# Attention scores of a pooled-attention and MLP kernel: 64 pools by one matmul for both token kinds, 8 pools in column tiles, k through a transposing DMA

## The chip, the cores and the metric

The kernel runs on one core of a Trainium2 chip. The metric is device time in microseconds (us), median of the runs of one program; a profile gives in addition the span from the first to the last instruction, about 1.8 us less. A core has TensorE (PE; the loads of its stationary operand, `lhsT` in the code, are shown apart, as PEld), VectorE (DVE), ScalarE (ACT), GpSimd (POOL) and SyncE (SP, which issues DMAs). A `q` after an engine's name (SPq, POOLq) stands for the DMA issues in its queue.

## The reference

Eight batches of eight heads, 576 tokens, head dimension 64. Keys and values are averaged over groups of eight tokens (72 pools), each token attends to the 72 pools of its head, and the result, 4608 tokens of 512, goes through an MLP with a tanh-gelu.

```python
k_p = k.reshape(B, H, Sp, pool, D).mean(axis=3)        # pool = 8, Sp = 72
v_p = v.reshape(B, H, Sp, pool, D).mean(axis=3)
scores = (1/sqrt(D)) * matmul(q, k_p.transpose(0, 1, 3, 2))
attn = softmax(scores)
x = matmul(attn, v_p)                                   # then to [B*S, H*D]
out = gelu_tanh(x @ w_in) @ w_out                       # 512 -> 2048 -> 512
```

## The kernel before

The nine groups of 512 tokens of the MLP run one after the other on TensorE. Each group has a first stage, 64 matmuls with w_in whose results, in banks of PSUM (the memory that these matmuls write), ScalarE takes through gelu, and a second stage, 64 matmuls with w_out. The attention of the next batch is woven into the second stage. Even and odd tokens lie in the two halves of the partitions of qT (64 rows of the head dimension each), so a score matmul takes pooled keys that are zero in the other half: 2 token kinds x 8 heads = 16 score matmuls a batch.

```python
def qk(b, c, pr, bank):                     # c: token kind, pr: pair of heads
    for e in range(2):
        h = 2 * pr + e
        n = pool_rows(pr)                   # 72 or 128
        nc.tensor.matmul(out=PS[:n, bank + e, :CH]...,          # CH = 288 tokens
                         lhsT=kTs[b % 2][c][:, h, :n],
                         rhs=qTs[b][:, h // 4, :, h % 4 * 32:h % 4 * 32 + 32], ...)

def trans_k(b, bank):                       # pooled k: five transposes by TensorE,
    trans_k_mm(b, bank)                     # then twelve copies by VectorE
    for e in range(2):
        trans_k_copy(b, e, bank)
# ... cut: exponentials (ACT), av (values, 16 matmuls), norm (ln, ln, exp), mult
```

The softmax here doesn't subtract the row's maximum and nothing guards it: scores larger than these inputs give would overflow.

## Time and profile before

| | before |
|---|---|
| median of 3 runs | 308.13 us |
| profiled span | 306.1 us |
| TensorE busy, mean granted clock | 97%, 1.00 |
| one period (first stage + second stage), batch 3 to batch 5 | 31.84 us |
| of it second stage (attention woven in) | 17.75 us |
| start of the second w_in stage to the end | 250.3 us |

The lines behind this are in the prediction below. A "period" is read from the chain that ended last, printed in order of time: it turns from the line of the w_in matmuls to the line of the w_out matmuls once in each period.

### The profile page before, as it was taken

Reading aid. Unit: us, or ns where it says so; the run is one execution under the profiler, and the core shown is the slowest. Engines: PE = TensorE matmul, PEld = TensorE weight load, DVE = VectorE, ACT = ScalarE, POOL = GpSimd, SP = SyncE. Lnnn points to the kernel's source line nnn. Section 1 sums busy time; section 2 is a strip of 40 time slices with the busy share of each in tenths; the row PEclk is TensorE's granted clock in tenths of the full one; section 3 lists DMA queues with packets and bytes.
Section 4 is the critical chain, followed back from the end, with each engine's and each line's share of the span. In section 5 each row is a group of like instructions: output and inputs, shape, how many; then the busy total and the mean of one; then the engine's idle time right before and its main releaser. Section 6 shows DMA issues by size and latency. Waiting matters only on the chain.

```text
span 306.1 us, 4354 instructions
## 1 busy us (share of the span) xinstructions
PE 296.8 (97%) x1528; PEld 157.6 (51%) x1557; DVE 150.5 (49%) x336; ACT 219.0 (72%) x402; POOL 35.0 (11%) x67
## 2 busy tenths in 40 slices
PE   8999899999999999999999999999999999999994
PEld 3555455555555555555555555555555555445543
DVE  5885757572577057805682559245932630120012
ACT  1687489867987798779977898789868986206500
POOL 7102002305003200320014000400000000000000
PEclk9999999999999999999999999999999999999999
DMA  7999987977955962696159827672101210121022
GB/s 221 266 254 264 227 171 139 310 168 184 257 138 113 278 154 53 118 279 154 35 112 250 181 61 103 203 153 71 35 1 36 59 44 0 36 70 35 2 68 69
DMA packets 30806, 41.12 MB, mean 134 GB/s; under 512 B 18176, under 2 KB 18432, under 8 KB 29888
## 3 DMA queue, kind: packets, MB, share of 16 engines
q0 software_dynamic: 7568, 24.38, 33.7%
q1 hardware_dynamic: 22528, 15.14, 21.1%
q10 hardware_dynamic: 688, 1.31, 1.3%
q8 instruction: 12, 0.20, 0.3%
q14 instruction: 10, 0.08, 0.1%
HBM read 36.70 MB, written 9.44 MB: 151 GB/s over the span
## 4 chain that ended last, share of the span: by engine, by line
PE 87%; DMA 11%; issue 1%; ACT 0%; DVE 0%; POOLq 0%
PE PS L344 40%; PE PS L335 37%; DMA qb<-in_q_dram 11%; PE PS L238 5%; PE PS L260 4%; PE PS L173 1%; PE PS L203 0%; ACT e L246 0%; ACT ld L268 0%; ACT ld L267 0%; DVE osb L353 0%; POOLq L550 0%
## 5 line engine op out<-in xcount | busy, mean ns | idle before, releaser
L344 PE MATMUL PS<-w_out_b,gT 128*128 128x512 bf16 (+2 forms) x577 | 133.9, 373 | 0.7
L335 PE MATMUL PS<-xT,w_in_b 128*128 128x512 bf16 x563 | 126.6, 379 | 0.7
L341 ACT ACTIVATE gT<-PS 128x512 bf16<-128x512 f32 x144 | 81.2, 603 | 48.1 <-PE PS L335 48.0
L335 PEld LDWEIGHTS <-w_in_b 128*128 128x128 bf16 x576 | 64.7, 113 | 57.2
L344 PEld LDWEIGHTS <-gT 128*128 128x128 bf16 x592 | 57.0, 97 | 55.7 <-issue 0.4
L353 DVE COPY osb<-PS 128x512 f32<-128x512 f32 (+2 forms) x37 | 25.1, 677 | 98.2 <-PE PS L344 78.6
L278 DVE TENSOR_TENSOR xT<-PS,rc 64x288 bf16<-64x288 f32 x112 | 50.9, 455 | 31.7 <-ACT rc L270 27.5
L246 ACT ACTIVATE e<-PS 72x576 bf16<-72x576 f32 (+1 forms) x64 | 41.0, 647 | 8.8 <-PE PS L238 7.9
L238 PE MATMUL PS<-qT,kT 128*72 128x288 bf16 (+1 forms) x128 | 25.8, 286 | 0.9 <-ACT qT L213 0.6
L270 ACT ACTIVATE rc<-ld 128x288 f32<-128x288 f32 x56 | 24.8, 444 | 1.8
L313 ACT ACT_TABLE_LOAD x17 | 21.8, 1283 | 4.3 <-issue 4.1
L267 ACT ACTIVATE ld<-PS 64x288 f32<-64x288 f32 x56 | 22.8, 408 | 1.3
L268 ACT ACTIVATE ld<-PS 64x288 f32<-64x288 f32 x56 | 22.5, 402 | 1.4
L260 PE MATMUL PS<-e,vp 72*128 72x288 bf16 (+1 forms) x112 | 23.1, 286 | 0.0
L138 DVE TENSOR_TENSOR kt<-kt 128x1280 f32<-128x1280 f32 (+5 forms) x18 | 18.9, 1048 | 7.6 <-DMA kt<-in_v_dram 4.6
L238 PEld LDWEIGHTS <-kT 128*72 128x72 bf16 (+1 forms) x128 | 13.2, 105 | 15.1 <-DVE qT L215 1.2
L453 POOL COPY gate<-qT 1x2 bf16<-1x2 bf16 x6 | 1.0, 174 | 138.5 <-DMA qT<-qb 138.5
L138 DVE TENSOR_TENSOR vt<-vt 128x1024 f32<-128x1024 f32 (+1 forms) x16 | 15.3, 956 | 1.7 <-DMA vt<-in_v_dram 1.4
L183 DVE COPY kT<-PS 64x288 bf16<-64x288 bf16 (+2 forms) x48 | 13.0, 318 | 6.2 <-PE PS L173 6.0
L260 PEld LDWEIGHTS <-vp 72*128 72x128 bf16 (+1 forms) x112 | 11.0, 98 | 3.8
L365 PE MATMUL PS<-idle 128*128 128x512 bf16 x32 | 10.4, 468 | 1.6 <-DVE idle L126 1.2
L76 POOL DMA_DIRECT2D kt<-in_v_dram x14 | 8.0, 586 | 0.1
(48 smaller groups left out, 88.8 us busy)
## 6 DMA issues: line engine op xcount, KB each, us to landing
out_dram<-osb SPq DMA_DIRECT2D x140, 64.0 KB
kt<-in_k_dram POOLq DMA_DIRECT2D x7, 1024.0 KB, 6.0
vt<-in_v_dram POOLq DMA_DIRECT2D x12, 512.0 KB, 8.7
qb<-in_q_dram POOLq DMA_DIRECT2D x7, 576.0 KB, 11.8
w_in_b<-in_moe_w_in_dram POOLq DMA_DIRECT2D x2, 1024.0 KB, 16.8
w_out_b<-in_moe_w_out_dram POOLq DMA_DIRECT2D x4, 512.0 KB, 19.3
vt<-in_v_dram SPq DMA_DIRECT2D x3, 512.0 KB
kt<-in_k_dram POOLq DMA_DIRECT2D x7, 128.0 KB, 6.0
```

The costliest lines, as they stand in the source:

```text
L138: nc.vector.tensor_tensor(out=o, in0=a, in1=b, op=ALU.add)
L238: nc.tensor.matmul(out=PS[:n, bank + e, :CH].rearrange("j (t p) -> j t p", p=32), lhsT=kTs[b % 2][c][:, h, :n], rhs=qTs[b][:, h // 4, :, h ...
L246: nc.scalar.activation(out=e[:n], in_=PS[:n, bank:bank + 2, :CH], func=ACT.Exp, scale=1.0 / 64.0)
L260: nc.tensor.matmul(out=PS[:, bank + x, :CH], lhsT=window(vps[b % 2][:n], 2 * pr + x), rhs=e[:n, x, :], start=True, stop=True)
L267: nc.scalar.activation(out=ld[0:64], in_=PS[64:128, bank, :CH], func=ACT.Ln)
L268: nc.scalar.activation(out=ld[64:128], in_=PS[0:64, bank + 1, :CH], func=ACT.Ln)
L270: nc.scalar.activation(out=rc, in_=ld, func=ACT.Exp, scale=-1.0)
L278: nc.vector.tensor_tensor(out=xT[rows, pr, col:col + CH], in0=PS[rows, bank + x, :CH], in1=rc[rows], op=ALU.mult)
L335: nc.tensor.matmul(out=PS[:, h_bank(g, fo), c0:c1], lhsT=w_in_b[fo // 8][:, ko, q * 512 + j:(q + 1) * 512:4], rhs=xT[:, ko, r0 + c0:r0 + c ...
L341: nc.scalar.activation(out=gTs[g][:, fo, :], in_=PS[:, h_bank(g, fo), :], func=ACT.Gelu_apprx_tanh)
L344: nc.tensor.matmul(out=PS[:, bank, c0:c1], lhsT=gTs[g][:, fo, r * 128:(r + 1) * 128], rhs=w_out_b[:, fo, c0:c1], start=(fo == 0), stop=(fo ...
L353: nc.vector.tensor_copy(out=osb[:, c0:c1], in_=PS[:, bank, c0:c1])
```

## The change

In batches 2 to 7 one stationary tile of 128 columns holds 64 pools of a head twice, for even and for odd tokens, so one matmul gives both: 8 in place of 16. The last 8 pools of all heads and both kinds, the remainder, come from eight matmuls of 16 rows. Four of them write to four column tiles (outputs that start at rows 0, 32, 64 and 96), meant to run side by side. Their exponentials must end up in rows 64 to 71 below the 64 others; VectorE moves the even rows, a DMA the odd ones. The pooled k is transposed by a DMA, not by TensorE.

```diff
+    KX = 2
+    def trans_k_dma(b):
+        kxs[b] = bp.tile([128, 2 * H + 2, 64], BF16, name="kx", bufs=1)
+        nc.sync.dma_start_transpose(out=kxs[b], in_=kz.rearrange("p h e c -> p (h e c)"))
+    def rem_scores(b):
+        kf = kxs[b].rearrange("p b j -> p (b j)")
+        for h in range(H):
+            i, x = h % 4, h // 4
+            nc.tensor.matmul(out=PS[32 * i:32 * i + 16, 6 + x, :CH].rearrange("j (t p) -> j t p", p=32),
+                             lhsT=kf[:, 2 * H * 64 + h::H], rhs=qTs[b][:, x, :, 32 * i:32 * i + 32],
+                             start=True, stop=True)
+    def rem_expo(b):
+        r = ep.tile([128, 2, CH], BF16, name="er", bufs=1)
+        nc.scalar.activation(out=r, in_=PS[:, 6:8, :CH], func=ACT.Exp, scale=1.0 / 64.0)
+        for i in range(4):
+            nc.vector.tensor_copy(out=eT[64:Sp, i:H:4, 0, :], in_=r[32 * i:32 * i + 8])
+            nc.sync.dma_start(out=eT[64:Sp, i:H:4, 1, :], in_=r[32 * i + 8:32 * i + 16])
+    def main_scores(b, pr):                 # ... two matmuls of 128 rows a pair, both kinds
+    def main_expo(b, c, pr):                # ... 64 rows, two heads
...
-            first += [(late, ko) for ko in range(3)]
-            first += [(fo, 3) for fo in rest + [late]]
+            first += [(fo, ko) for fo in (late, 4) for ko in range(3)]
+            first += [(fo, 3) for fo in rest + [late, 4]]
...     (cut: loads of k and v in another order and after the eT DMA, q transposed in the
...      stage before use, other bank numbers, kT and vp of 72 rows, v of batch 1 in halves)
```

## The prediction

> **What bounds the kernel now.** I read the busy times first, then the chain that ended last in order of time, then the stages one by one, then the ScalarE and SyncE timelines inside one of them. The page says that TensorE is the engine that is full, and at the full clock:
>
> ```profile
> PE 296.8 (97%) x1528; PEld 157.6 (51%) x1557; DVE 150.5 (49%) x336; ACT 219.0 (72%) x402; POOL 35.0 (11%) x67
> PEclk9999999999999999999999999999999999999999
> ```
>
> A busy TensorE row alone proves little, so I cut the span into the repeating period: one group of 512 tokens, 64 matmuls with w_in (L335), then 64 with w_out (L344) with the attention of the next batch between them. The boundaries are where the chain turns from L335 to L344. Two of them, start, length and busy time per engine (PE, PEld, DVE, ACT, POOL):
>
> ```profile
> 101.71:133.55 31.84, 31.68 (x163) 16.99 (x165) 17.60 (x39) 26.63 (x50) 4.40 (x8) 1.00 0.65 157
> 165.39:197.23 31.84, 31.68 (x163) 16.99 (x165) 17.60 (x39) 26.64 (x50) 3.67 (x7) 1.00 0.64 136
> ```
>
> 31.68 of 31.84 us are matmul, so a period should be the sum of its matmuls. The chain gives their streaming cost (start, us, what):
>
> ```profile
> 96.25 0.28 PE PS L173 x5
> ...
> 101.71 1.29 PE PS L344 x6
> 103.00 0.24 PE PS L238 x2
> 103.25 1.73 PE PS L344 x8
> 104.98 0.24 PE PS L238 x2
> 105.22 0.25 PE PS L260 x2
> ```
>
> A 512-column matmul is 1.73/8 = 0.216 us, a 288-column one (scores L238, values L260) 0.245/2 = 0.1225 us, and the five k transposes are 0.28 us together. The "mean ns of one" (379, 286) includes the pipeline's tail and must not be multiplied. Check: 128 x 0.216 + 32 x 0.1225 + 0.28 = 27.65 + 3.92 + 0.28 = 31.85, against 31.84. So any TensorE time removed from a period is time saved, as long as nothing takes its place. The nearest candidate is ScalarE in the w_out stage; its timeline near the end of one stage:
>
> ```profile
> 117.06 0.65 ACT L246 ACTIVATE e<-PS 128x576 bf16<-128x576 f32 x1
> 117.74 0.41 ACT L267 ACTIVATE ld<-PS 64x288 f32<-64x288 f32 x1
> 118.17 0.40 ACT L268 ACTIVATE ld<-PS 64x288 f32<-64x288 f32 x1
> 118.60 0.44 ACT L270 ACTIVATE rc<-ld 128x288 f32<-128x288 f32 x1
> 119.07 0.41 ACT L267 ACTIVATE ld<-PS 64x288 f32<-64x288 f32 x1
> ```
>
> No idle is noted, and it ends at 120.39, 0.93 us after TensorE has gone on to the next L335 stage (119.46 in the chain). ScalarE is full in this stage and has its rest in the other.
>
> **What the Trainium skill says.** "TensorE: Matmul & The Clock Gate", Part 3, gives 2.38 times for three column tiles of 32 at 512 columns: matmuls in different column groups run together. No run so far shows it: in the kernel before no matmuls lie beside each other in four column tiles. "TensorEngine Tiling (Array Packing)", Key Properties, adds that changing the tiling mode drains TensorE; that isn't visible here either. "VectorE: DVE Perf Modes", TRN2 errata, gives 58 + FD/Accel cycles at 0.96 GHz for a copy inside SBUF; a bf16 copy of 576 elements at 4x is then an estimate of (58+144)/0.96 = 0.21 us. The kernel before has no such copy. [...]the transposing DMA of q: issued from 91.89 to 94.60, its waiter ran at 96.58, 1.98 us later:
>
> ```profile
> 91.89 2.71 SPq L223 DMA_TRANSPOSE qT<-qb  x1
> ```
>
> **The change part by part.** It acts on the six batches from 2 to 7, in six of the nine periods; batches 0 and 1 keep the old scores.
>
> Removed from TensorE per period: 16 score matmuls become 8 (one stationary tile carries the 64 pools for even and for odd tokens), 8 x 0.1225 = 0.98 us; the five k transposes, 0.28 us. Sum 1.26 us. The values matmuls stay 16.
>
> Added to TensorE: eight matmuls of 16 rows x 288 columns in four column tiles, for the last 8 pools. At one after the other they are 0.98 us; at a speed-up of 2.4 they are 0.41 us, and I add 0.14 us for the two changes of mode, an estimate of mine. I take 0.55 us.
>
> ScalarE: the eight exponentials of 576 columns stay eight (64 rows for 72 or 128, and duration follows columns: 72 and 128 rows both took 647 ns), plus one for the remainder, 0.65 us. Now I lay the second stage out by hand, from its start. The table load ends at 2.0 us (103.64 in the trace, stage start 101.6). Remainder exponential 2.05 to 2.72; first main pair to 3.39 and 4.06. VectorE's copies of the even tokens take 0.21 each, heads 0 and 1 need two: ready at 3.2. The first values matmuls stand behind 13 w_out matmuls: 2.81 + 0.55 + 0.25 = 3.6: no wait. The second ones stand at 22 x 0.216 + 0.55 + 3 x 0.245 = 6.04; the normalisation of pair 0 (1.29 us) and one exponential come first, so their input is ready at about 6.1 to 6.2. I take 0.15 us of waiting. After that ScalarE has two normalisations queued and runs back to back, with perhaps 0.3 us lost at the sixth, and ends at 2.05 + 9 x 0.67 + 8 x 1.29 + 0.3 = 18.7 us. TensorE ends the stage at 13.82 + 0.55 + 0.98 + 1.96 + 0.15 = 17.5. ScalarE thus overhangs 1.2 us, the last multiply lands about 2.3 us into the next stage. There the change moves to 15 matmuls (fifth tile included) that need no last head pair, 15 x 0.216 = 3.2 us: 0.9 us of room.
>
> DMA for odd tokens: four issues on SyncE at 0.69 us each (its vp<-kp issues have a median of 687 ns), from 2.75 on; with 2 us to land the last is there at 7.5. The first user of odd tokens is at 28 x 0.216 + 0.55 + 5 x 0.245 + 0.15 = 8.0. Hidden, narrowly.
>
> k by DMA: loads go after that, from 7.6 us in the second stage. Before, k took 6.0 us to land, and k, v and q together about 15 (issue 97.11; q 11.7 after 100.58). So k is there before the stage ends and q 5 us into the next. VectorE adds k after its last multiply: 1.49 + 0.83 + 2 x 0.42 + 0.22 plus a copy of 0.3, from 2.3 to 6.0. Transposing k, half of q's rows: an estimate of 1.35 us of issue, then q's 2.7, then 2 to land: all there at 12.1. First use is at 13.82 + 0.43 = 14.2. Hidden with 2 us of room.
>
> Before the six periods: fewer memsets and smaller copies, v of batch 1 loaded later and added in halves, one DMA wait placed in ScalarE's queue. TensorE waits there for q of batch 1:
>
> ```profile
> 33.73 0.45 PE L203 MATMUL PS<-identb,qb 128*128 128x128 bf16 x5 [1.41 <-DMA qb<-in_q_dram]
> ```
>
> The bytes ahead of that load remain, so what is won earlier is lost at this wait. I count 0.
>
> Sum per period: 1.26 - 0.55 - 0.15 = 0.56 us, six times 3.4 us: 308.1 - 3.4 = 304.7 us.
>
> **The rivals.** First, the column tiles don't run together. Then the remainder costs 0.98 plus drains, the gain per period is about 0.1, and the time is 307.5. For it: nothing in the trace shows concurrency. Against: the skill's measurement. Second, ScalarE becomes the bound: if it loses 1 us more in the second stage, TensorE waits at the last head pair in the next, and up to 0.5 us per period is given back: 306 to 308. For it: 18.7 us of work in a 17.5 us stage. Against: over the whole period its 26.6 + 0.65 = 27.3 us leave 4 us. Third, a DMA comes late: q or k transposed after 14.2, or the odd rows after 8.0. Each us late is 6 us in all: 309 to 313. For it: chains of four steps with 0.5 to 2 us of room, where the kernel before had q transposed a period ahead. Against: DMA is at 0.6 to 0.7 busy, and the loads end before the transposes. Fourth, all goes best, remainder 0.30 and no wait: 6 x 0.96 = 5.8, 302.4.
>
> **Range and chances.** The middle is the sum, 304.7; the low end is a little below the best case (the start may win some tenths), the high end is the first two rivals together. Over 2% faster means under 302.0, beyond the best case; over 2% slower, above 314.3, needs the third rival at its worst. Range 301.7 to 308.2.
>
> **What would show it.** Right: periods of about 31.3 us; eight remainder matmuls starting within 0.4 us; no DMA among the waits of TensorE in the w_out stage; ScalarE ending just over 1 us into the next stage; VectorE's 8-row copies at 0.2 us. Wrong: remainder matmuls 0.12 us apart (first rival); TensorE waiting for VectorE's multiplies at the start of the L335 stage (second); TensorE waiting for kx, qT or eT from a DMA (third). Copies of 0.7 us would move the first values matmuls by 0.5 us each period, and a start longer than before by over 1 us would also make it wrong.

## The result

The changed kernel took 302.91 us (median of 4 runs, 302.34 to 303.77), the kernel before 307.81 us in the same rounds. The ratio is 0.9848, 95% interval 0.9813 to 0.9882. The gain is 4.9 us, by the ratio 1.5%: clear of the interval, though less than the 2% from which a run is called faster here. 3.4 us had been predicted, and the time lies inside the stated range.

| | before | after |
|---|---|---|
| profiled span | 306.1 | 301.2 |
| one period | 31.84 | 31.08 |
| first stage / second stage | 14.09 / 17.75 | 13.81 / 17.26 |
| start of the second w_in stage to the end | 250.3 | 245.7 |

The page of the kernel after, busy times and clock:

```profile
PE 292.1 (97%) x1498; PEld 151.4 (50%) x1527; DVE 149.6 (50%) x299; ACT 216.6 (72%) x408; POOL 37.6 (12%) x67
PEclk9999999999999999999999999999999999999998
```

The shares hardly moved. TensorE is still the full engine, with less to do. The stages cut by time (start:end, length, then busy time of PE, PEld, DVE, ACT, POOL; the last three numbers are granted clock, DMA share and GB/s):

```profile
69.37:100.44 31.07, 30.91 (x158) 15.88 (x160) 17.66 (x35) 26.39 (x51) 4.55 (x8) 1.00 0.71 159
131.52:162.60 31.08, 30.78 (x158) 15.87 (x160) 17.66 (x35) 26.38 (x51) 4.58 (x8) 1.00 0.72 159
```

Every period of the six is 31.07 or 31.08 us long, 0.76 less than before, and six times that is 4.6 us. The other 0.3 us of the gain, 0.7 in the repetition a1 below, lie outside these periods. The chain at the start of a second stage, in order of time:

```profile
100.44 0.43 PE PS L405 x2
100.88 0.38 PE PS L296 x8
101.25 0.16 issue
101.41 0.81 PE PS L405 x3
102.22 0.24 PE PS L311 x2
102.47 1.51 PE PS L405 x7
103.98 0.25 PE PS L322 x2
```

L405 is w_out, L296 the eight remainder matmuls, L311 the new scores, L322 the values. The eight lie in 0.38 us. The "issue" after them is not a wait: four w_out matmuls stand there in program order and three are recorded, so one record is missing. To avoid that I count from start to start: 100.44 to 102.22 is 1.78 us and holds six w_out matmuls (6 x 0.216 = 1.29) and the remainder, which thus cost 0.49 us all told.

Where ScalarE ends a second stage and begins the next first stage, which starts at 117.71 here:

```profile
118.39 0.45 ACT L332 ACTIVATE rc<-ld 128x288 f32<-128x288 f32 x1
118.86 1.28 ACT L373 ACT_TABLE_LOAD   x1
121.20 3.04 ACT L402 ACTIVATE gT<-PS 128x512 bf16<-128x512 f32 x6 [1.06 <-PE PS L396]
```

It ends 1.13 us into the next first stage and, after loading the table for gelu, still waits 1.06 us for TensorE: it isn't the bound. The multiplies that follow its normalisations end later, because VectorE first copies a result of w_out:

```profile
117.75 0.69 DVE L410 COPY osb<-PS 128x512 f32<-128x512 f32 x1 [1.15 <-PE PS L405]
118.47 1.88 DVE L340 TENSOR_TENSOR xT<-PS,rc 64x288 bf16<-64x288 f32 x4
```

The last of them ends at 120.35, 2.64 us into the stage. SyncE's transposing DMAs, for the batch used from 131.89 on, and VectorE's eight-row copies (line, form, count, busy and mean ns):

```profile
124.19 1.44 SPq L178 DMA_TRANSPOSE kx<-kz  x1
126.31 2.96 SPq L256 DMA_TRANSPOSE qT<-qb  x1
```
```profile
L304 DVE COPY eT<-er 8x576 bf16<-8x576 bf16 x24 | 7.3, 302 | 39.9 <-ACT er L302 39.4
```

### The profile page after: what moved, and what is told of

Same layout as the page of the kernel before. It is cut to its first block, busy times and chain, and to the rows that moved or that the text cites. A ratio compares the mean times of both kernels' runs of the same rounds, so it can differ in the third digit from the quotient of the medians.

```text
span 301.2 us, 4348 instructions
## 1 busy us (share of the span) xinstructions
PE 292.1 (97%) x1498; PEld 151.4 (50%) x1527; DVE 149.6 (50%) x299; ACT 216.6 (72%) x408; POOL 37.6 (12%) x67
## 4 chain that ended last, share of the span: by engine, by line
PE 87%; DMA 7%; POOL 1%; DVE 1%; issue 1%; ACTq 0%; ACT 0%; DVEq 0%; POOLq 0%
PE PS L405 41%; PE PS L396 38%; DMA kt<-in_v_dram 7%; PE PS L322 4%; PE PS L311 2%; DVE kt L150 1%; PE PS L296 1%; PE PS L287 1%; PE PS L267 1%; POOL w_in_b L114 0%; POOL qb L95 0%; PE PS L236 0%; ACTq L183 0%; ACT gT L402 0%; POOL kt L74 0%
## 5 line engine op out<-in xcount | busy, mean ns | idle before, releaser
L405 PE MATMUL PS<-w_out_b,gT 128*128 128x512 bf16 (+2 forms) x575 | 138.0, 373 | 0.9 <-issue 0.2
L405 PEld LDWEIGHTS <-gT 128*128 128x128 bf16 x592 | 56.5, 97 | 52.5 <-issue 1.7
L410 DVE COPY osb<-PS 128x512 f32<-128x512 f32 x35 | 24.2, 691 | 64.7 <-PE PS L405 61.4
L317 ACT ACTIVATE eT<-PS 64x576 bf16<-64x576 f32 x48 | 30.7, 640 | 0.6
L304 DVE COPY eT<-er 8x576 bf16<-8x576 bf16 x24 | 7.3, 302 | 39.9 <-ACT er L302 39.4
L322 PE MATMUL PS<-eT,vp 72*128 72x288 bf16 x96 | 19.7, 285 | 0.1
L150 DVE TENSOR_TENSOR vt<-vt 128x1024 f32<-128x1024 f32 (+3 forms) x18 | 17.1, 952 | 1.1 <-DMA vt<-in_v_dram 0.8
L322 PEld LDWEIGHTS <-vp 72*128 72x128 bf16 x96 | 9.5, 98 | 11.3
L274 ACT ACTIVATE e<-PS 72x576 bf16<-72x576 f32 x16 | 9.9, 644 | 2.6 <-PE PS L267 2.4
L311 PE MATMUL PS<-qT,kx 128*128 128x288 bf16 x48 | 9.8, 286 | 0.0
L82 POOL DMA_DIRECT2D kt<-in_k_dram x12 | 7.5, 630 | 2.1 <-issue 2.1
```

Of the source, the lines that this page charges most:

```text
L150: nc.vector.tensor_tensor(out=o, in0=a, in1=b, op=ALU.add)
L317: nc.scalar.activation(out=eT[0:64, 2 * pr:2 * pr + 2, c, :], in_=PS[64 * c:64 * c + 64, 2:4, :CH], func=ACT.Exp, scale=1.0 / 64.0)
L322: nc.tensor.matmul(out=PS[:, bank + x, :CH], lhsT=window(vps[b % 2], 2 * pr + x), rhs=eT[:, 2 * pr + x, c, :], start=True, stop=True)
L405: nc.tensor.matmul(out=PS[:, bank, c0:c1], lhsT=gTs[g][:, fo, r * 128:(r + 1) * 128], rhs=w_out_b[:, fo, c0:c1], start=(fo == 0), stop=(fo ...
L410: nc.vector.tensor_copy(out=osb, in_=PS[:, bank])
```

## The experiments

All runs are correct unless said. "Rest" is the time from the start of the second w_in stage to the end of the profiled span; "period" the distance of two second stages.

| run | ratio to before (95%) | rest, us | period, us |
|---|---|---|---|
| before | 1 | 250.3 | 31.84 |
| a1_changed_again | 0.9841 (0.9816 to 0.9866) | 245.7 | 31.08 |
| e1_never | 1.0003 (0.9983 to 1.0023) | 251.8 | 31.85 |
| e2_from_five | 0.9903 (0.9884 to 0.9921) | 247.9 | 31.85, then 31.08 |
| e6_transposes_back | 0.9953 (0.9938 to 0.9968) | | 31.35 |
| e3_rem_twice | 0.9902 (0.9876 to 0.9927) | 247.5 | 31.32 |
| e4_rem_pairs | 0.9841 (0.9826 to 0.9856) | 245.7 | 31.09 |
| e5_rem_one_tile | 0.9972 (0.9957 to 0.9987) | 250.0 | 31.80 |
| e7_even_by_dma | 1.0178 (1.0161 to 1.0195) | 256.4 | |
| e8_scalar_one_more | 0.9863 (0.9830 to 0.9897) | 245.6 | 31.08 |
| e9_scalar_three_more | 1.0023 (0.9984 to 1.0062) | 250.6 | 31.85 to 31.98 |
| e10_move_later | 0.9832 (0.9816 to 0.9849) | 245.7 | 31.08 |
| e11_from_one | 1.0170 (1.0151 to 1.0189) | | |

My theory was that the gain is TensorE work removed in six batches and nothing else. The rivals were the other edits, column tiles that don't run together, ScalarE, and late DMAs.

**a1_changed_again**: no edit.

> The changed kernel unaltered, so that the others of this call can be compared with it on the same chip. Expected 0.985 of the kernel before, a profiled span of 301.2 us, periods of 31.08 us.

The span was 300.7, the rest 245.7 as in the first profile. So the rest repeats to a tenth while the start moved by half a microsecond.

**e1_never**: are the other edits worth anything?

```diff
-    KX = 2
+    KX = 8          # and the old early load for every batch that exists
```

> The changed kernel, but no batch uses the new scores: all keep the old 16 score matmuls and the five transposes. Theory A (the whole gain is TensorE work removed in six batches, the other edits are worth 0.2 us): span 301.2 + 6 x 0.76 = 305.8 to 306, ratio 0.998 to 1.000 of the kernel before. Rival (a good part of the gain comes from the other edits: start, banks, memsets, order of the first matmuls): span 304 or less, ratio under 0.995.

The time went back to that of the kernel before, and each later period to 31.85. The span, 306.8, is a little over the expected one because of one wait in the first of these batches, which the kernel before doesn't have (the timeline of TensorE: start, length, instructions, idle before and its releaser):

```profile
73.82 0.42 PE L287 MATMUL PS<-e,vp 72*128 72x288 bf16 x2 [1.17 <-DMA vp<-kp]
```

That small DMA stands behind the transposing DMA of q in SyncE's queue. So the run shows that without the new scores the gain in the periods is gone. It doesn't show that the other edits are worth nothing: its total equals that of the kernel before within 0.2%, but its profile holds that wait of 1.17 us, and its start was 0.7 us shorter (55.05 us against 55.78), so that a gain and a loss may hide each other. What the new start is worth stays open, within about 1 us.

**e2_from_five**: does the gain scale with the batches?

```diff
-    KX = 2
+    KX = 5
```

> The new scores only for batches 5, 6 and 7. Theory A: half the gain, span 301.2 + 3 x 0.76 = 303.5 us, and each new period 31.08, each old one 31.84. Rival (a fixed gain or loss at the changeover): span off 303.5 by over 0.7 us.

The rest is 2.2 us over the changed kernel's and 2.4 under that of before: half and half. The expected span of 303.5 became 302.9, since this run's start was the shorter by half a microsecond. There is no cost at the changeover.

**e6_transposes_back**: what were the k transposes worth?

```diff
-                plan = {0: kk, 7: vv[:1], 8: vv[1:]}
+                plan = {0: kk, 7: vv[:1], 8: vv[1:], 9: [lambda: trans_k_mm(nb, 4)]}
```

> Five transposes of pooled k are put back into each w_in stage of batches 2 to 7, their result unused. Theory A (TensorE has no free time, so they cost what the chain shows, 0.28 us each batch): span +1.7 us, 302.9. Rival (the transposes were hidden or nearly free between other matmuls): +0.3 us or less.

The span grew by 3.5 us, twice what I expected, but the periods, 31.35 against 31.08, say 0.27 each as they should. The rest of it is mostly two waits, one that my edit brought with it in batch 2, where VectorE hadn't yet written what the transposes read, and one in batch 5 for q's transposing DMA:

```profile
64.89 0.28 PE L212 MATMUL PS<-identb,kp 128*128 128x128 bf16 x2 [1.07 <-DVE kp L150]
165.39 0.44 PE L296 MATMUL PS<-qT,kx 128*16 128x288 bf16 x8 [0.55 <-DMA qT<-qb]
```

So the total of this run says little; the periods that have no wait confirm 0.27 to 0.28 us.

**e3_rem_twice**: how much of the remainder's cost is matmul?

```diff
             at(2, rem_scores, nb)
+            at(2, rem_scores, nb)
```

> The eight remainder matmuls are issued twice over. If they run together in four column tiles, eight more cost two waves of 288 columns, 2 x 0.12 = 0.24 us a batch, 1.5 us in all: span 302.7 us; the rest of the 0.37 us is then a cost of the change of mode, paid once. If they ran one after the other at some shorter time of their own, the second eight would cost 0.37 again: +2.2 us, 303.4. At the full 0.12 each: +5.8 us, 307.0.

Eight more cost 0.24 us a period, two waves of 0.1225 (a wave is four matmuls that run together): four column tiles run fully side by side. Of the 0.49 us that the remainder takes, the other 0.24 are paid once, whatever the number of matmuls. That fits a drain, a wait until the matmuls under way are done, at each of the two changes of tiling mode; no run separates it from other fixed costs, such as a first weight load. The rest grew by 1.8, not 1.5: in one period TensorE waited 0.28 us for q's transposing DMA:

```profile
163.70 0.69 PE L296 MATMUL PS<-qT,kx 128*16 128x288 bf16 x16 [0.28 <-DMA qT<-qb]
```

**e4_rem_pairs**: does the order matter?

```diff
-        for h in range(H):
+        for h in (0, 4, 1, 5, 2, 6, 3, 7):
```

> Only the order of the eight remainder matmuls changes: heads 0, 4, 1, 5, 2, 6, 3, 7, so that each two neighbours share a column tile. If concurrency comes from neighbours in different tiles, a pair must run one after the other while the next pair may join its second half: about five waves for two, 0.6 to 0.75 us in place of 0.37: span +1.4 to +2.2 us. Rival (the order does not matter[...]): within 0.3 us of 301.2.

Nothing changed, and my expectation fell:

```profile
100.32 0.45 PE L296 MATMUL PS<-qT,kx 128*16 128x288 bf16 x8
```

Neighbours in program order may share a column tile and still the eight take two waves: in the trace's single records, as in those of the changed kernel, four start within 0.02 us, and the other four 0.15 us after them. How TensorE does that (a queue for each tile, or a window of reordering) no run here tells.

**e5_rem_one_tile**: are the tiles the cause at all? Its output is wrong, which doesn't matter for the time.

```diff
-            nc.tensor.matmul(out=PS[32 * i:32 * i + 16, 6 + x, :CH]...
+            nc.tensor.matmul(out=PS[0:16, 6 + x, :CH]...
```

> Wrong result on purpose: all eight remainder matmuls write the first column tile. If column tiles are what makes them cheap, they now take 8 x 0.12 = 0.98 us plus the change of mode, +0.6 to +0.75 us a batch: span +3.7 to +4.5 us, 304.9 to 305.7, and most of the change's gain is gone. Rival (16-row matmuls are cheap wherever they go): within 0.5 us of 301.2.

The same matmuls in one column tile, from the timelines of TensorE, the changed kernel's run a1 first and this run after it:

```profile
100.26 0.45 PE L296 MATMUL PS<-qT,kx 128*16 128x288 bf16 x8
```
```profile
100.77 1.17 PE L296 MATMUL PS<-qT,kx 128*16 128x288 bf16 x8
```

0.72 us longer, 4.3 us over six batches: without concurrency nearly the whole gain is gone, and the 16-row matmul is as dear as one of 128 rows. By the same sum, 0.49 + 0.72 = 1.21 = 8 x 0.1225 + 0.23: again a fixed part of about 0.24.

**e7_even_by_dma**: is moving by VectorE needed?

```diff
         for i in range(4):
-            nc.vector.tensor_copy(out=eT[64:Sp, i:H:4, 0, :], in_=r[32 * i:32 * i + 8])
+            nc.sync.dma_start(out=eT[64:Sp, i:H:4, 0, :], in_=r[32 * i:32 * i + 8])
+        for i in range(4):
             nc.sync.dma_start(out=eT[64:Sp, i:H:4, 1, :], in_=r[32 * i + 8:32 * i + 16])
```

> The even tokens' remainder rows go by DMA like the odd ones, even first, in place of VectorE's copies. Theory: a row by DMA is there about 2.7 to 3.0 us after the exponential (two issues of 0.77 and 1.3 to land, from the trace), the first values matmuls want it 0.8 us after, so TensorE waits 1.8 to 2.3 us each batch and the odd rows, four issues later, cost some more: span +11 to +16 us. Rival (the copies by VectorE are only a convenience, other waits are as long): under +4 us.

10.7 us more in the rest, just below the range, and the waits are where they should be, two in each batch. Those of batch 2:

```profile
73.25 0.28 PE L323 MATMUL PS<-eT,vp 72*128 72x288 bf16 x1 [1.18 <-DMA eT<-er]
73.88 0.28 PE L323 MATMUL PS<-eT,vp 72*128 72x288 bf16 x1 [0.35 <-DMA eT<-er]
```

The waits for these rows are 7.5 us in the six batches, 1.25 a batch where I had expected 1.8 to 2.3. Three more, 1.3 us in all, are for q's transposing DMA, which comes after them in SyncE's queue.

The rows that are wanted first have to go by the engine that takes 0.3 us a copy; a DMA can carry those that are wanted 4 us later.

**e8_scalar_one_more** and **e9_scalar_three_more**: has ScalarE room?

```diff
+    def extra(n):
+        for _ in range(n):
+            d = ep.tile([128, 512], BF16, name="xd", bufs=1)
+            nc.scalar.activation(out=d, in_=idle, func=ACT.Exp, scale=1.0 / 64.0)
...
+                if x == [7]:                # before the last normalisation
+                    at(m, extra, 1)         # e9: 3
```

> One more exponential on ScalarE (512 columns, about 0.6 us, result unused) before the last normalisation of each of the six batches. Theory A (ScalarE ends about 1.3 us into the next stage and then waits 1.06 us for its first gelu, so there is room for one): within 0.5 us of the changed kernel. Rival (ScalarE already bounds the period): +0.6 x 6 = 3.6 us.

> Three more of them, about 1.8 us a batch, over the room of 1.06 us. Theory A: the gelus start 0.8 us late; TensorE has 20 matmuls (4.3 us) before it needs a bank back, and the last multiply is wanted 3.2 us into the stage but lands at about 4.6 in the batches where the next group takes it, so 0.5 to 1.4 us a batch are lost: span +3 to +8 us. Rival B (ScalarE's slack over the whole period, 4 us, absorbs it): within 1 us.

One more exponential costs nothing: the rest is 245.6. (The span, 301.7, is longer by the start alone.) Three more, 1.94 us, cost 0.77 to 0.9 us a period. TensorE waited for the last multiply, at the point that the prediction named as the danger, in two of the six periods only; in the other four it waited for a gelu (the first line is of a timeline, the others are sums of waits: us, times, longest):

```profile
90.83 10.74 PE L401 MATMUL PS<-xT,w_in_b 128*128 128x512 bf16 x49 [0.74 <-DVE xT L345]
```
```profile
PE PS L401 <- ACT gT L407: 2.4, 4, 0.6
PE PS L401 <- DVE xT L345: 1.5, 2, 0.7
```

The code says why. A group has 512 tokens and a batch 576, so from batch 4 on the next group no longer reads what the last multiply of its batch writes. What TensorE then needs first is a bank that a late gelu has to empty.

So ScalarE's room in a period is over 0.6 and under 1.9 us, and 1.0 to 1.2 by the difference of what was added and what was lost (1.94 - 0.9 and 1.94 - 0.77).

**e10_move_later**: in the first profile of the changed kernel TensorE waited 0.39 us for a gelu in the first stage of all, because ScalarE stood at a DMA of its own queue.

```diff
-                plan = {0: kk[:-1], 7: kk[-1:], 12: tq[:1], ...
+                plan = {0: kk[:-1], 10: kk[-1:], 12: tq[:1], ...
```

> The DMA of v's last pools of batch 1, which stands in ScalarE's queue after the eighth gelu and held ScalarE from 29.4 to 31.2 us, is moved three gelus later, after the eleventh. Theory: TensorE's wait of 0.39 us for a gelu there goes, if q of batch 1 has landed by then: 0.3 to 0.6 us won, ratio to the kernel before 0.983. Rival (TensorE then reaches the q transposes before the load has landed): no change.

No gain that the intervals could show (0.9832 against 0.9841). In run a1 the unchanged kernel had no such wait either: it comes and goes with the moment at which k of batch 1 lands. With the DMA later, TensorE waited 0.8 us for VectorE's sums of k in its place (0.5 in a1) and 0.2 for q, much as the rival said. My expectation of 0.3 to 0.6 us fell.

**e11_from_one**: would one more batch gain as much?

```diff
-    KX = 2
+    KX = 1
-    load_k(1, [nc.gpsimd])
+    load_k_dma(1)
-        nc.sync.dma_start_transpose(out=kxs[b], ...
+        (nc.scalar if b == 1 else nc.sync).dma_start_transpose(out=kxs[b], ...
     # and the side work of the first group adapted, its early load left out
```

> The new scores for batch 1 as well (its k transposed by a DMA on ScalarE's queue, since SyncE's queue still carries v; its q still transposed by TensorE). Theory A: one more batch at 0.6 (score matmuls) + 0.28 (transposes): 0.9 us less from the start of the first w_in stage to the end, about 0.3% faster than the changed kernel, ratio to before 0.981. Rival: the first 40 us are bound by DMA (its share is over 1.0 there), so that the transposed k comes after 37.4 us and TensorE waits for it: no gain, or a loss of 1 to 3 us.

The rival held, and worse than it said: 10.0 us slower than the changed kernel's median, 10.5 slower than in a1. Two stretches of this run (columns as above; the third from last is the granted clock, then DMA share) and the wait between them:

```profile
35.00:40.00 5.00, 3.42 (x28) 2.04 (x26) 1.41 (x3) 1.65 (x4) 0.00 (x0) 1.00 1.06 250
45.00:50.00 5.00, 3.40 (x16) 1.33 (x17) 1.86 (x5) 1.03 (x2) 0.00 (x0) 0.50 0.09 19
```
```profile
46.60 0.68 PE L296 MATMUL PS<-qT,kx 128*16 128x288 bf16 x8 [5.92 <-DMA kx<-kz]
```

The DMA engines are full until 45 us, and the transposed k comes 12.8 us after its issue at 33.8. TensorE waits 5.92 us, and after so long a wait its clock is granted at 0.50 for the next 5 us. By an estimate these two make 8.5 us of the loss, the wait and half of the 5.2 us from 46.6 until the clock is full again; a wait of 1.58 us for a gelu before them is most of the rest. In the Trainium skill, "TensorE: Matmul & The Clock Gate", Part 1, describes this state, half the clock after an idle window of about 3.4 us; the trace agrees in that the clock was halved after this wait and not after that of 1.58 us, while the 3.4 us themselves no run tests. No version that I ran beats the changed kernel beyond the noise.

## Why the prediction was right, and where not

**TensorE sets the period.** Right. e1, e2 and the periods show that the gain is that of six batches, 0.76 to 0.77 us each, and e6 that 0.28 us of TensorE put back cost that much. The periods are 31.08 us where the prediction named about 31.3.

**The remainder at 0.55 us.** Nearly right in sum, wrong in its parts, and that the two errors offset each other was luck. It costs 0.49: the waves 0.245, not 0.41, since four tiles gave the full factor of four (e3) where I had taken over a factor measured with three, and the fixed part, which I had put down to the changes of mode, 0.24, not 0.14 (e3, e5).

**0.15 us of waiting at the second values matmuls.** This step failed; there is no wait there. I had given each exponential 0.67 us from start to start; the first three of a stage started 0.58 apart in the trace (102.39 to 104.14), so that the input was there in time. With both terms put right the sum is 0.98 + 0.28 - 0.49 = 0.77 a batch and 4.6 in all, and that is what the periods gained; the 1.2 us between this and the predicted 3.4 are these two terms. The rest of the 4.9 us lies outside the periods and isn't explained.

**ScalarE overhangs by 1.2 us with 0.9 to spare.** Right in size: it ended 1.13 us into the next stage, and e8 and e9 put the room between 0.6 and 1.9 us. The path was right in part. The last multiply landed at 2.64 us, not 2.3, because a copy stood before it on VectorE, so that 0.6 us were left before TensorE's 3.2. In e8 it landed at 2.63 although ScalarE was later: VectorE, not ScalarE, set the time there. And only two of the six groups need that multiply (e9).

**The odd rows by DMA are hidden, narrowly.** Right: the waiter of the last of them ran at 107.43, the first values matmuls of odd tokens began at 107.79, and those need only the first two of the four DMAs.

**k and q transposed with 2 us of room.** The direction was right, the size wrong. kz was ready 6.4 us into the first stage, where I had 6.0, q's issue began 0.7 us after k's had ended, and it took 2.96 us. It ended at 129.27; with the 1.98 us to land of the kernel before this is an estimate of 131.25, against a first use at 131.89. The room is 0.6 us, and four runs went over it: e3 in one period by 0.28, e6 in one by 0.55, e11 in one by 0.38, e7 in three by 0.2 to 0.7.

**The start counts 0.** Open: e1's ratio is 1.0003, but with a wait of its own (see there). The second w_in stage began at 55.78 us before and between 54.7 and 56.1 in the profiles with the new start, so less than a microsecond can't be told.

**The copies at 0.2 us.** They took 0.30. That did no harm, because only two of four stand before the first values matmuls.

## What to carry to other kernels

If the busiest engine's instructions add up to the period, price a change by what it takes off that engine, and count matmuls by the distance of their starts, not by the duration shown. Small matmuls in four column tiles cost a quarter each, but a visit to that mode has a price of its own, so collect them in one place. What has to change partitions should go by the engine that is quick for the rows wanted first and by DMA for the rows wanted later, and the room of each such chain should be read again from the new trace: here it was a third of what was planned, and one batch earlier, with the DMA engines full, it was gone.

## What the Trainium skill lacked or had wrong

- "TensorE: Matmul & The Clock Gate", Part 3, gives a measured speed-up for three column tiles, 2.38 times, and none for four. Here eight more matmuls of 288 columns in four tiles cost 0.24 us a batch, against 8 x 0.1225 = 0.98 one after the other: a factor of 4, beside the fixed part.
- The same part says that matmuls start and end in strict program order. With neighbours in the same column tile (e4) that would need five waves, 0.61 us; the period stayed at 31.09 against 31.08 us. For column tiles in this kernel it doesn't hold as it stands.
- "TensorEngine Tiling (Array Packing)", Key Properties, says that a change of tiling mode drains TensorE and gives no figure. Going into column tiles and back cost 0.24 us here beyond the matmuls, in e3 and e5 alike; that it is the drain alone no run shows.
- "VectorE: DVE Perf Modes", TRN2 errata, gives 58 cycles as the fixed part of a copy in SBUF, which made 0.21 us; 302 ns were measured for 576 bf16 elements. Its remark below the table, a fixed part of about 150 cycles, gives (150 + 144) / 0.96 = 306 ns and is the one to use.
- No page gives, for trn2 and by size, the time that the issue of a transposing DMA holds its queue. In the changed kernel's first profile it was 1.3 to 1.4 us on SyncE for 64 rows of 2304 elements and 2.9 to 4.1 for the 128 rows of q (2.7 to 2.9 in the kernel before); on ScalarE's queue, with the DMA engines full (e11), 3.72 us for the 64 rows.
